# Late weight loads in held pieces, and a new instruction order, in an attention and gated-FFN kernel

## The chip, the cores and the metric

The kernel runs on one core of one Trainium2 chip. The metric is device time in microseconds; the time before is the median of three runs. Beside it stands one profiled execution, from which all durations of instructions come.

## The reference

One transformer block with adaptive layer norm, in bf16, for 2048 rows of width 448. Cut to what matters:

```python
mod = (silu(c) @ w_mod)                     # 448 -> 6 x 448: sa, ca, ga, sb, cb, gb
h = layernorm(x) * (1 + ca) + sa
x = x + ga * A(h)                           # attention, 16 heads of 28, 4 segments of 512 rows
h = layernorm(x) * (1 + cb) + sb
x = x + gb * B(h)                           # (sigmoid(h @ w_gate) * (h @ w_up)) @ w_down, 448 -> 1792 -> 448

# A, per segment s and head:
logits = q @ k.T * scale + causal mask;  a_dot = softmax(logits) @ v
a_mem = (phi(q) @ M) / (phi(q) @ z + 1e-6)  # memory of the segments before
o = g * a_mem + (1 - g) * a_dot             # g = sigmoid(beta)
M += phi(k).T @ v;  z += phi(k).sum(rows)   # then o @ wo
```

## The kernel before

The rows are four segments of 512, each of four tiles of 128. For each segment there are these stages: layer norm of x (`ln1`), projection to q, k and v (`proj`; QK at L861, V at L873), attention in pairs of head groups (`attention`: logits at L942, exp on ScalarE at L956 and L962, masks on VectorE or GpSimd at L972 and L969, probabilities times v, "PV", at L997), the update and the reading of the memory (`memory`: L905, reading at L1012), the output projection with the second layer norm (`wo_ln2`, L1064) and the FFN (`ffn`: gate/up at L1086, tanh at L1091, product at L1093, down at L1105). Segments overlap freely.

Nothing in this order is written by hand. Every piece of work is a node with a duration, dependencies, buffers ("slots") and a priority. `Graph.run` plays the nodes through a model of the five engines, takes at each moment the ready node of highest rank plus priority, and emits the instructions in the order found. The priorities are the long table `PRM`, one number for each node of a kind. So the instruction order on every engine changes when a number of the model or the table changes. Where the plan leaves TensorE (PE) idle for over 465 ns, `fillers` puts matmuls of an identity matrix (L1129, 512 columns) into the gap. They compute nothing that is used.

The model of transfers: `moved` gives each of two rings (SP's and ACT's queue) a time at which it is done, at `ALONE` bytes per ns for one ring and `SHARED` for each of two. A load of over 100,000 bytes isn't placed until its ring has less than `BACKLOG` ns left (`ready_at`). On the chip nothing enforces that: SP issues its instructions in order, each waiting only for its own inputs, for its buffers, and for the completion of an earlier DMA whose semaphore it reuses.

Weights, x and w_mod are loaded whole into SBUF by `load` (all at L470; `load_x`, `load_wm`, `load_half` call it). The first nine (x of segment 0, c, the first two sixths of w_mod in halves, wq and wk) are followed by x of segment 1, wv and the late loads: x of segments 2 and 3, wo, beta, the other four sixths of w_mod, w_gate and w_up, w_down. The late ones are 0.1 to 0.8 MB in one DMA each. wq and wk land in the room of w_down (`wqk_st`) and are copied into padded form (`pad`, L684), each half of the rows by itself. The modulation columns come from small matmuls (`mod_cols`, L647), rows of `rep` from L667; `rep` is multiplied into wo and w_down (`scaled`, L737).

SP's queue also carries the work of the pipeline: DMA transposes of phi(k) for the memory (`pk`, L897), of normalized x to hT (L746; segments 1 and 2 of the first norm are transposed on PE instead, L801), shifts of hT by half a partition range (L763, L766), and the stores (L1114). All of them stand in one order with the loads.

Of the kernel before, what the change touches and what calls it, by code (L numbers as in the profile page):

```python
# [13 lines left out]
P = 128  # L14
# [5 lines left out]
BACKLOG = 4000  # L20
SLACK = 250
INF = float("inf")
ALONE, SHARED = 245.0, 128.0

PRM = {
    "ld": (369044, 307344, 893451, -617209, 30545, -391681, 769994, 478104, 1506413, 246196, -153238, 622995, -344888,
        224457, 782907, 740955, -44415, -487957, -94697, 242376, -73834, 194363),
    "ws": (-205973, 384123, 102965, -72595, 270215, -214773, -562464, -199188, 289943, -1205891, -728759, -1210279,
        -853673, -1075673, -350090, -1112115, -456678, -2097630),
    "pj": (-809354, -799212, -1778232, -1222127, -1304831, -1422717, -1211794, -1974074, -2582402, -1784797, -1731699,  # L30
        -1432997, -787233, -1335907, -2169951, -2822676, -1343114, -2573680, -1822391, -2040683, -923550, -2107391,
        -2184641, -1772924, 241705, 15, 907154, 1122271, 852108, -24519, -377776, -196722, -768290, -3128, -829073,
        1122250, 558630, -504600, 262888, 119667, 425019, 241126, -781718, 138521, -173254),
    "ev": (910059, 583732, 734901, 348841, 415278, 361124, 390341, -350495, 605466, 1248190, 724478, 252990, 351177,
        -1060760, 99560, -339224, -579824, -480446, -952199, -1451478, -1228059, -1526733, -1188205, -2509101,
        1191510, 22486, -84708, -371324, -169064, -114692, -190608, -244213, 362489, -343011, -1096591, -1537722,
        -1239794, -971924, -673075, -1689010, -798158, -1411682, -1153882, -1348954, -1025849, -1118869, 14420,
        -1271712),
    "ln1": (52067, 457878, 689734, -177302, 167731, 288133, 181471, 312244, 85018, -190473, 836826, 733058, 908845,
        372065, 683673, -149642, 344424, 242833, 314959, 501854, 448238, 419745, 542826, -964768, -865865, -230782,  # L40
        109468, 724418, 41927, 192489, 345817, 251112, 277411, 939082, 576541, -160264, -329797, 306498, 897168,
        766275, 2031348, 501806, 1766664, -69744, -39732, 324817, 229652, -54789, 3426, 289366, 830871, -47867,
        504740, 17973, -332856, -194935, -270092, 657322, -1107999, 525892, -759213, -396386, 733594, 749680, 106946),
    "lg": (1903571, 2022275, 1868112, 2492143, 2383876, 2586210, 2118683, 1882073, 2434369, 1886752, 1265668, 1340630,
        739152, 1303984, 1344026, 2536971, 1764119, 1241619, 1417148, 940850, 2512247, 2373585, 1883725, 1755289,
        2246130, 2550777, 1280778, 1713172, 2980793, 1929447, 297802, 204360, 890058, 334188, 793051, -100783, 18628,
        609572, 158909, 686064),
    "ex": (3564046, 3415132, 3230920, 3886453, 2313177, 2404922, 3927356, 3471590, 4587747, 4505003, 1453103, 1197683,
        1419481, 1801405, 2800617, 2386818, 3055996, 2191047, 3943526, 3948848, 560113, 365875, 32592, -221844,
        348045, 873648, 6784, -481362, -603239, 302311, 769230, 1239061, 267867, 1564753, 637563, 638151, 281869,  # L50
        1036958, -746944, -317314),
    "mask": (949863, 968922, 1025971, 1653190, 2119047, 1920918, 1193528, 1060185, 968830, 1168662, 761261, 2129529,
        312432, 868757, 101127, 1364527, 250510, 1113337, 577913, 1276705, -40254, 536688, 1489338, 1029585, 1609834,
        1409696, 1024136, 1708955, 1607140, 1259647, 859837, 927495, 2427991, 2719449, 1857647, 2000572, 2270880,
        2012462, 1984328, 1632846, 1905041, 2121280, 2009590, 1692404, 1761962, 1685634, 1411239, 2185621, 793486,
        1192963, 1059030, 2141224, 1191945, 832868, 1583163, 551125, 210455, 441087, 634838, 930737, -10241, 608473,
        -235122, -86120),
    "pv": (2024955, 1705170, 2121590, 2726403, 185538, -734262, -103118, 865308, 606370, 149540, -254295, 990181,
        1635364, -434629, 60743, -536729),
    "t": (4021845, 3284741, 3378831, 2837695, 3791130, 4028739, 3373723, 4088406, 4456495, 4394824, 4316511, 4464689,  # L60
        3610155, 4144735, 3351270, 3974440, 3926537, 3705196, 4153703, 3844887, 12885, 665101, 305886, 211984,
        -280121, -239218, -459123, -25417, -320069, -238085, -287382, -666766, -111888, -448350, 124538, -369246,
        -737071, -213905, 1061166, -157374, -171996, -1478, -128551, -487876, 557914, 87380, -870478, 593318, 1660752,
        1126315, 1432537, 1325506, 1564262, 1782156, 1087670, 323061, 1594629, 2449642, 1918056, 2171760, 1574669,
        2005941, 1301827, 463032, 1435304, 1616727, 1524119, 1834373, 1839720, 1166831, 1239971, 1945109, 1293771,
        563554, 691509, 578776, -1494877, -458256, -787761, -824978, -1302790, -1050010, -1163239, -485195, -1937716,
        -1556847, -1977134, -1339590, -1591507, -1970508, -2635238, -2513520, -2630457, -2795043, -1814184, -1961049,
        -2590543, -2115038, -2828279, -2902843, -1841705, -1839436, -1490899, -2503918),
    "mem": (-761151, -31405, -1250643, -869816, -54841, -648031, -672042, -515182, -241137, -578229, -847415, -707828,
        -701013, -644854, -766583, -909362, -815994, -721421, -1269986, -748082, -793279, -932656, -656490, -671383,  # L70
        -536295, -654941, -333962, -463382, 380173, -204560, -289039, 209087, 66392, 502939, 1382865, -131351,
        -234499, 66498, 1231588, -58380, 599180, 376114, 33108, 526362, -607611, -195402, 218825, -912746, 360064,
        375098, 307889, 1040252, -29441, -60290, -266616, -302473, -408987, 589363, -40653, 114816, 45042, -209977,
        -1122178, 261467, -391896, -1074153, 480972, -311029, -174412, -372529, -189426, -300491, 544003, -226374,
        -196848, -136121, -149339, 611266, -694186, 132091, -189423, 189256, 125668, 100891),
    "wo": (1549545, 297144, 804041, 702070, 1410707, 1336115, 626526, 817071, 2184614, 2146397, 2195436, 3865766,
        -25540, 876630, -102149, -105363),
    "ln2": (1332947, 1273028, 1506731, 1286904, 124566, 995769, 1035016, 1551617, 1637288, 2670502, 1260360, 1672705,
        1429596, 1478613, 1276621, 1000534, 1279013, 729179, 2058679, 539528, 1161654, 664944, 1389903, -89914,
        1278040, 378904, 3125799, 2357638, 2948912, 3377722, 3084159, 1860920, 3172458, 4033052, 3001611, 3242704,  # L80
        3029696, 2951538, 3082954, 4190512, 4732975, 3146788, 3328802, 3364689, 3878089, 3501800, 3192639, 4423838,
        3895319, 3861042, 4240208, 3567222, 1208624, 928648, 1364166, 1658632, 1079427, 1126380, 804122, 330511,
        1687289, 665380, 16347, 868165, 774465, 1536304, 414383, 1917025, 1747624, 748313, 540321, 1319646, 1356096,
        2538213, 2029661, 1858805, 2001187, 1359124, -1285087, -2150644, -1723686, -1460713, -1619459, -1822046,
        -2048580, -2655047, -1898342, -2398157, -1965591, -2604854, -1591466, -2787155, -2631412, -2568863, -2435621,
        -3364265, -3599030, -2755780, -3191395, -3312191, -3255869, -2777146, -1945181, -2783150),
    "gu": (1883258, 2529781, 1813290, 2063698, 2907212, 2816880, 2759594, 3435519, 3657375, 4012953, 2379677, 3091622,
        2629540, 2690560, 4073697, -9991, 586451, 230677, -63569, 57047, 1016820, 159005, 1337820, 1174721, 600366,
# [23 lines left out]
        212024, 797709, -654264, -1385151, -216052, -431657, -526471, -392088, -1414877, -1357692, -1196457, -826264,  # L112
        -938840, -867425, -1377686, -1389691, -861918, -1830229, -1270960, -572877, -769492, -1156832, -2091094),
}
STAY = 84351
COST = {"ACT": 1.136, "DVE": 1.482, "POOL": 0.978}


# [220 lines left out]
def kernel(  # L339
# [17 lines left out]
    _, S, D = A_x.shape  # L357
# [805 lines left out]
```

## Time and profile before

| | |
|---|---|
| runs | 260.26, 261.92, 262.08 us; median 261.92 |
| profiled execution | 260.36 us, its span 258.6 us |
| mean granted PE clock | 0.993 |
| busy in the span | PE 238.2 us, VectorE (DVE) 196.7, ScalarE (ACT) 155.1, GpSimd (POOL) 36.8 |
| HBM | 11.07 MB read, 1.84 MB written |

Lines of a profile name the kernel's line, the engine, the operation and "out<-in" tiles; "x28" is a count; a bracket at the end is the time its engine stood idle before it and what ended that. In a timeline the first two numbers are start and length in us. The busy time of pipelined matmuls is modelled.

### The profile page before, as it was taken

The numbers are of one execution on the slowest core, as the hardware profiler recorded it, in microseconds if no ns is written. First come the engines' busy times: TensorE is split into PE (matmuls) and PEld (weight loads), VectorE is DVE, ScalarE is ACT, GpSimd is POOL, SyncE is SP. The second block draws the span as 40 slices with busy tenths as digits, with TensorE's granted clock in tenths as the row PEclk, the third lists the DMA queues.
The fourth block names the chain that finished last, engine by engine and source line by source line (L and its number), as shares of the span: only waits on it lengthen the run. The fifth ranks groups of instructions, "written<-read, shape, count | busy, mean of one in ns | idle before, by whom it ended". The sixth has DMA issues, their size and how long they took to land. (4 is left out here: it accounts for less than half of the span.)

```text
span 258.6 us, 6013 instructions
## 1 busy us (share of the span) xinstructions
PE 238.2 (92%) x2397; PEld 107.7 (42%) x2397; DVE 196.7 (76%) x499; ACT 155.1 (60%) x195; POOL 36.8 (14%) x91
## 2 busy tenths in 40 slices
PE   8769889979897999998979999899999999999994
PEld 3534545623332444433424444344444444454442
DVE  4489989987999998799998996669898754332431
ACT  5039969969988868898476558777431223022300
POOL 6204052300610000012500160000001300000000
PEclk9999999979999999999999999999999999999999
DMA  6999999993433010101354015201100330100011
GB/s 166 208 220 216 216 174 241 227 160 62 114 63 94 20 24 0 23 4 20 77 68 103 4 29 73 71 3 35 38 0 0 63 92 4 53 18 3 0 37 37
DMA packets 29832, 19.78 MB, mean 76 GB/s; under 512 B 18347, under 2 KB 28268, under 8 KB 29804
## 3 DMA queue, kind: packets, MB, share of 16 engines
q1 hardware_dynamic: 29276, 18.77, 36.5%
q10 hardware_dynamic: 528, 0.63, 0.9%
q8 instruction: 19, 0.31, 0.5%
q14 instruction: 9, 0.07, 0.1%
HBM read 11.07 MB, written 1.84 MB: 50 GB/s over the span
## 5 line engine op out<-in xcount | busy, mean ns | idle before, releaser
L1086 PE MATMUL ps<-hT,wgu 64*128 64x512 bf16 x784 | 91.2, 377 | 2.7 <-DMA hT<-hT 1.3
L1091 ACT ACTIVATE tt<-ps 128x512 f32<-128x512 f32 x56 | 33.5, 597 | 58.9 <-PE ps L1086 56.5
L956 ACT ACTIVATE pT<-ps 128x2048 bf16<-128x2048 f32 x32 | 60.4, 1886 | 6.9 <-PE ps L942 6.9
L1086 PEld LDWEIGHTS <-wgu 64*128 64x128 bf16 x784 | 38.8, 94 | 50.8 <-issue 13.1
L1093 DVE SCALAR_TENSOR_TENSOR fT<-tt,ps 128x512 bf16<-128x512 f32 x56 | 38.1, 682 | 25.9 <-ACT tt L1091 25.8
L1105 PE MATMUL ps<-wd_sb,fT 128*128 128x448 bf16 x224 | 46.2, 353 | 0.0
L861 PE MATMUL ps<-hT,wqk 64*128 64x512 bf16 x224 | 28.1, 383 | 2.5 <-DVE hT L821 1.9
L1105 PEld LDWEIGHTS <-fT 128*128 128x128 bf16 x224 | 20.4, 98 | 22.7 <-issue 5.7
L969 POOL TENSOR_SCALAR_AFFINE_SELECT pT<-pT 128x512 bf16<-128x512 bf16 x17 | 10.9, 638 | 95.1 <-DVE aT L1020 39.7
L972 DVE TENSOR_TENSOR pT<-pT,cmask 128x512 bf16<-128x512 bf16 x47 | 18.4, 419 | 6.8 <-ACT pT L956 5.6
L595 DVE BATCH_NORM_STATS2 st<-x_sb 128x6 f32<-128x448 bf16 x32 | 19.7, 615 | 3.9 <-DMA x_sb<-in_A_x_dram 3.5
L603 POOL TENSOR_TENSOR rs<-rs,mhalf 128x1 f32<-128x1 f32 (+1 forms) x29 | 17.0, 586 | 2.4
L861 PEld LDWEIGHTS <-wqk 64*128 64x128 bf16 x224 | 10.7, 94 | 14.9 <-issue 5.5
L942 PE MATMUL ps<-qT,kT 28*128 28x512 bf16 (+3 forms) x256 | 16.1, 304 | 0.4 <-DVE hT L821 0.2
L602 POOL TENSOR_SCALAR rs<-mv 128x1 f32<-128x1 f32 (+1 forms) x29 | 6.6, 226 | 68.8 <-DVE mv L596 61.5
L1112 DVE TENSOR_TENSOR ot<-ps,x_sb 128x448 bf16<-128x448 f32 x16 | 9.8, 618 | 8.5 <-PE ps L1105 8.2
L962 ACT ACTIVATE pT<-ps 128x2048 bf16<-128x2048 f32 x8 | 15.0, 1877 | 0.9 <-PE ps L942 0.9
L997 PE MATMUL ps<-pT,vt 128*32 128x512 bf16 (+3 forms) x256 | 12.0, 302 | 2.1 <-DVE x_sb L1067 0.8
L1064 PE MATMUL ps<-wo_sb,oT 128*128 128x448 bf16 x64 | 13.3, 353 | 0.4 <-DVE wo_sb L737 0.2
L844 ACT CAST kT<-ps 128x512 bf16<-128x512 f32 x12 | 7.1, 593 | 8.0 <-PE ps L861 8.0
L608 DVE TENSOR_SCALAR xn<-x_sb,mv,rs 128x448 bf16<-128x448 bf16 x32 | 11.4, 389 | 0.6 <-POOL rs L603 0.5
L873 PE MATMUL ps<-wvv,hT 64*128 64x448 bf16 x112 | 11.8, 350 | 0.0
(95 smaller groups left out, 240.4 us busy)
## 6 DMA issues: line engine op xcount, KB each, us to landing
out_dram<-ot SPq DMA_DIRECT2D x16, 112.0 KB, 1.7
wgu<-in_B_w_gate_dram SPq DMA_DIRECT2D x3, 448.0 KB, 11.4
wgu<-in_B_w_up_dram SPq DMA_DIRECT2D x3, 448.0 KB, 16.0
hT<-hT SPq DMA_DIRECT2D x5, 256.0 KB, 3.2
hT<-hT SPq DMA_DIRECT2D x5, 192.0 KB, 2.7
x_sb<-in_A_x_dram SPq DMA_DIRECT2D x2, 448.0 KB, 15.6
wd_sb<-in_B_w_down_dram SPq DMA_DIRECT2D x2, 448.0 KB, 11.4
wvv<-in_A_wv_dram SPq DMA_DIRECT2D x2, 392.0 KB, 8.1
```

The costliest lines, as they stand in the source:

```text
L595: nc.vector.bn_stats(st_r[:, st.at, :], src)
L603: nc.gpsimd.tensor_tensor(r, r, mhalf[:, 0:w], ALU.pow)
L861: nc.tensor.matmul(pf(b), lhsT=w, rhs=piece(hT, i, half), start=(i == 0), stop=(i == NP - 1))
L942: nc.tensor.matmul(ps[:, lg.at + hs, o:o + nq], lhsT=kT_r[r, k.at, hcs[u], kb * P:(kb + 1) * P], rhs=qT_r[r, q.at, hcs[u], kb * P:L], star ...
L956: nc.scalar.activation(pT_r[:, pTs[units[0]].at, :, w0:w0 + L], ps_, AF.Exp, scale=scale)
L962: nc.scalar.activation(dst, ps_.rearrange("p h (u w) -> p u h w", u=2), AF.Exp, scale=scale)
L972: nc.vector.tensor_tensor(blk, blk, cmask[:].rearrange("p (o k) -> p o k", o=1).to_broadcast([P, 4, P]), ALU.mult)
L1064: nc.tensor.matmul(pf(b)[:, 0:D], lhsT=oT_r[:, oT.at, k, t * P:(t + 1) * P], rhs=wo_sb[:, k, :], start=(k == 0), stop=(k == NHC - 1))
L1086: nc.tensor.matmul(pf(b), lhsT=wgu[half * HR:(half + 1) * HR, chunk_of(i, half), fs], rhs=piece(hT, i, half), start=(i == 0), stop=(i == N ...
L1091: a = act(485, lambda gp=gp, tt=tt: nc.scalar.activation(tt_r[:, tt.at, :], pf(gp), AF.Tanh, scale=0.5), [n], use=[gp, tt], prio=pr("tanh" ...
L1093: f = dve(597, lambda up=up, tt=tt, ft=ft: nc.vector.scalar_tensor_tensor(fT_r[:, ft.at, :], tt_r[:, tt.at, :], 1.0, pf(up), op0=ALU.add, ...
L1105: nc.tensor.matmul(pf(b)[:, 0:D], lhsT=fT_r[:, fts[fc].at, t * P:(t + 1) * P], rhs=wd_sb[:, fc, :], start=(fc == 0), stop=(fc == NFC - 1))
```

## The change

Three edits, and what follows from them.

1. `load` ties each load from the tenth on to the third load ahead of it in the order of creation: it is a dependency of the node in the plan, and on the chip a semaphore wait of the issuing queue until that load has landed.
2. The late loads are cut into pieces: x in halves of a segment, w_mod in two or four pieces, w_gate and w_up by one chunk of 64 rows at a time (0.23 MB), w_down by two chunks (0.23 MB). Their order of creation is also changed.
3. The model's rates are lower (215 and 111 for 245 and 128), the backlog limit is taken out (the tie stands in its place), rings start at 2000 ns for 2600, the lags of the first loads are other ones, and `PRM`, `STAY` and `COST` are all new. So the order of instructions is another one on every engine.

The number of instructions of each kind stays, but for loads and for fillers (14 to 41). A few evacuations, modulations, masks and scalings move between ACT, DVE and POOL.

```diff
-BACKLOG = 4000
+BACKLOG = 1e9
...
-ALONE, SHARED = 245.0, 128.0
+ALONE, SHARED = 215.0, 111.0
...
-STAY = 84351
-COST = {"ACT": 1.136, "DVE": 1.482, "POOL": 0.978}
+STAY = 96324
+COST = {"ACT": 0.957, "DVE": 0.883, "POOL": 0.756}
...
-        self.ring = {"SP": 2600.0, "ACT": 2600.0}
+        self.ring = {"SP": 2000.0, "ACT": 2000.0}
...
             n.fn(n.eng) if len(n.durs) > 1 else n.fn()
+            if n.move is not None:
+                n.name = block[was].name
+            if n.tie is not None:
+                tc.add_manual_dep(block[was], n.tie.name, mybir.DependencyInfo(
+                    mybir.DependencyClass.Sync, mybir.DependencyReason.DATA), reason="few loads wait at a time")
...
-    EARLY, LATE = -1500, 1200
+    EARLY, LATE = -900, 500
+    DEPTH, UNTIED = 3, 9
+    loads = []
...
-        return add(eng, 450 if size < 200000 else 640, fn, deps, prio=prio, use=use, take=take, move=size, lag=lag)
+        tie = loads[-DEPTH] if len(loads) >= UNTIED else None
+        n = add(eng, 450 if size < 200000 else 640, fn, [*deps, tie], prio=prio, use=use, take=take, move=size, lag=lag)
+        n.tie = tie
+        loads.append(n)
+        return n
...
-                    HR * (c1 - c0) * n * 2 * 1.15, (), prio, lag=lag)
+                    HR * (c1 - c0) * n * 2 * 1.03, (), prio, lag=lag)
...
-    W_qk = [load_half("SP", wqk_st, half, w, first(6 + half), lag=-200) for half, w in enumerate((A_wq, A_wk))]
+    W_qk = [load_half("SP", wqk_st, half, w, first(6 + half), lag=900) for half, w in enumerate((A_wq, A_wk))]
...
-    load_x("SP", 2 * TPS, 3 * TPS, ld())
-    load_wm(("SP",), 2, 1, fT_flat[:, 2 * NK * D:], ld())
+    load_x("SP", 2 * TPS, 2 * TPS + 2, ld())
+    load_x("SP", 2 * TPS + 2, 3 * TPS, ld())
...
-    load_wm(("SP",), 3, 2, fT_flat, ld())
-    W_gu = [load_half("SP", wgu, half, w, ld(), c0, c1) for c0, c1 in ((0, 2), (2, 4), (4, 6), (6, 7))
-            for half, w in ((0, B_w_gate), (1, B_w_up))]
-    load_x("SP", 3 * TPS, 4 * TPS, ld(), [n_warm, n_pads, *n_vpad, *n_vone, *n_opad])
-    load_wm(("SP",), 5, 1, fT_flat[:, 3 * NK * D:], ld())
+    load_wm(("SP", "SP"), 2, 1, fT_flat[:, 2 * NK * D:], ld)
+    W_gu = []
+
+    def load_gu(c0, c1):
+        for c in range(c0, c1):
+            W_gu.extend(load_half("SP", wgu, half, w, ld(), c, c + 1) for half, w in ((0, B_w_gate), (1, B_w_up)))
+    load_gu(0, 2)
+    load_wm(("SP",) * 4, 3, 2, fT_flat, ld)
+    load_gu(2, 4)
+    load_x("SP", 3 * TPS, 3 * TPS + 2, ld(), [n_warm, n_pads, *n_vpad, *n_vone, *n_opad])
+    load_x("SP", 3 * TPS + 2, 4 * TPS, ld(), [n_warm, n_pads, *n_vpad, *n_vone, *n_opad])
+    load_gu(4, NC)
+    load_wm(("SP", "SP"), 5, 1, fT_flat[:, 3 * NK * D:], ld)
     l_wd = []
-    for f0, f1 in ((0, 4), (4, 7), (7, 11), (11, 14)):
-        l_wd += [load("SP", wd_sb[:, f0:f1, :], B_w_down.rearrange("(fc p) n -> p fc n", p=P)[:, f0:f1, :],
-                      (f1 - f0) * P * D * 2, W_p if f0 < NC else (), prio=ld())] * (f1 - f0)
+    for f0 in range(0, NFC, 2):
+        l_wd += [load("SP", wd_sb[:, f0:f0 + 2, :], B_w_down.rearrange("(fc p) n -> p fc n", p=P)[:, f0:f0 + 2, :],
+                      2 * P * D * 2, W_p if f0 < NC else (), prio=ld())] * 2
```

The changed kernel's lines stand 12 to 20 further down than the old ones (the QK matmul, L861 before, is L881 after).

## The prediction

> **What bounds the kernel now.** I read the page first, then timelines of TensorE (PE), VectorE (DVE), ScalarE (ACT) and the SyncE queue (SPq), then windows.
>
> ```profile
> span 258.6 us, 6013 instructions
> ...
> PE 238.2 (92%) x2397; PEld 107.7 (42%) x2397; DVE 196.7 (76%) x499; ACT 155.1 (60%) x195; POOL 36.8 (14%) x91
> ...
> GB/s 166 208 220 216 216 174 241 227 160 62 114 63 94 20 24 0 23 4 20 77 68 103 4 29 73 71 3 35 38 0 0 63 92 4 53 18 3 0 37 37
> ```
>
> PE is busy for 92% of the span; the loads run at some 216 GB/s (slices of 6.5 us) until 57 us. The window from the first tanh of the gate/up stage (83.95) to the end shows the rest (columns: length; busy PE, weight load, DVE, ACT, POOL; clock, DMA share, GB/s):
>
> ```profile
> 83.95:258.60 174.65, 166.72 (x1544) 73.05 (x1540) 126.14 (x290) 91.98 (x112) 14.42 (x32) 1.00 0.15 33
> ```
>
> Of 174.65 us PE is idle 7.93, and 3.36 of those follow the last matmul. So this stage is PE's, and loads can matter only ahead of 84 us. There PE shows these waits for transposes (pk) that share the SP queue and its DMA engines with the loads:
>
> ```profile
> 52.31 0.28 PE L905 MATMUL ps<-vt,pk 128*32 128x32 bf16 x16 [0.42 <-DMA pk<-pq]
> ...
> 54.31 0.28 PE L905 MATMUL ps<-vt,pk 128*32 128x32 bf16 x16 [1.40 <-DMA pk<-pq]
> ...
> 67.65 0.28 PE L905 MATMUL ps<-vt,pk 128*32 128x32 bf16 x16 [0.68 <-DMA pk<-pq]
> ```
>
> The transpose for the 54.31 line was issued at 47.99, 6.3 us earlier, behind loads; the page's median for all twelve is 3.4 us. After that idle time PE's granted clock (after the busy time in these rows) fell:
>
> ```profile
> 56.00:57.00 1.00, 1.00 (x8) 0.50 0.71 86
> 57.00:58.00 1.00, 1.00 (x7) 0.50 0.60 128
> ```
>
> The microseconds beside these stand at 0.75 and 0.55, so the clock cost 0.25 + 0.5 + 0.5 + 0.45 = 1.7 us. What loads cost through transposes is thus 2.5 us of waiting and 1.7 of clock: at most 4.2 us to be gained.
>
> **Part 1, the start.** The changed order (compared instruction by instruction) moves three things ahead of the first query/key matmul (QK). Before:
>
> ```profile
> 8.76 2.63 PE L801 MATMUL ps<-ident,xn 128*128 128x128 bf16 x32
> 11.23 2.03 PE L647 MATMUL ps<-silu,pT 112*128 112x32 bf16 x64
> 13.11 0.81 PE L1129 MATMUL ps<-ident 128*128 128x512 bf16 x3
> 15.79 0.61 PE L861 MATMUL ps<-hT,wqk 64*128 64x512 bf16 x4 [1.88 <-DVE hT L821]
> 16.67 3.18 PE L861 MATMUL ps<-hT,wqk 64*128 64x512 bf16 x26 [0.27 <-ACT hT L823]
> ```
>
> The 32 transposes (L801) use the time in which w_mod is still landing (issued 1.72 and 2.02, 7.8 and 7.9 us to landing: 9.92). In the changed order 32 of the 64 column matmuls stand ahead of the transposes, so PE stands still until 9.95. Then 32 columns 1.0 (half of 2.03), transposes 2.6, 32 columns 1.0: 14.5. DVE's columns 0.2 and semaphores: hT begins at 14.8 (15.20 before), and its five parts with ACT's two between take 3.1 as before (15.20 to 18.32): 17.9. Now the second move: DVE copied two of wk's four pads before hT (14.28, 0.69 for two); now all four follow hT, so QK starts at 17.95 + 0.35 + 0.1 = 18.4, not 15.79. Third, 14 fillers (idle matmuls that the order puts in PE gaps, 0.20 each by 0.81 for three with overlap, 0.21) fill 14.5 to 17.4, inside the wait, so they cost nothing; without that cover 2.9. Before, the first two heads' QK came in bits as hT landed, the first exp began at 20.63. Now 28 QK (26 in 2.98 at 20.14, so 3.2) and 0.3 logits give 22.1, with the same lead to exp **22.5: 1.9 us late**. DVE is not late: its pads and zeroing were done meanwhile.
>
> **Part 2, up to the first gate/up.** ACT between 20.63 and 83.95 is busy 56.2 and idle 7.2 (63.32 less 56.16 in the window). Counting ACT's order in the same stretch, the changed one has 2 exps more (1.77 apart by their starts), 5 evacuations fewer (0.48), 1 e, 1 hT and 1 epsilon evacuation fewer (0.53, 0.70, 0.58), both LN multiplies gone to other engines (0.72 each), one small tanh more: 3.5 - 2.4 - 1.8 - 1.4 + 0.1 = -2.0. So 22.5 + 54.2 + 7.2 = **83.9**, with the waits as before. PE's order gives bounds. I sum it by groups with their spacing in dense rows (QK and gate/up 0.1155 each, V 0.105, 0.33 a group of logits, 0.66 for 16 PV, wo 0.196, filler 0.21): 57.2 us from the first QK to the end of the first 14 gate/up (24 fillers in them), 56.4 before (10 fillers). Before, 67.9 us passed (15.8 to 83.7), 11.5 over the work. 18.4 + 57.2 + 11.5 = 87.1 if nothing is saved; less 2.9 for 14 more fillers that stand where waits were, and less the 4.2 above, 80.0. ACT's value lies between and I take it.
>
> **Part 3, the loads.** 38 pieces now go out by SP after the first ones, each waiting for the third ahead of it. A 112 KB load landed in 2.4 to 2.6 us; 0.2 MB more than that at 216 GB/s gives some 3.0, three in flight: 1.0 us a piece, 0.2 MB/us, near the 216 of before. From x of segment 1 (now held until w_mod lands, 9.9; DVE needs it at 19) the list runs to 55 to 59 us; before it ended at 57. I cost it at nothing up to 84 us; cover: x of segment 3, W_gate/up and W_down are needed after 50, 80 and 110 us. Behind each held piece in SP's queue stand pk transposes (four, between pieces) and then eight hT transposes; DVE gives their inputs at about 40, 41, 48, 52 and 60 us (its work summed in its new order, plus the 8 to 10 us by which DVE lags its own sum in the old one), which is what SP will wait for. Bounds: at 1.29 us a piece (37.5 us from 14 to 51.5 over 29 pieces) the queue is late for the second w_mod load that rep needs, and each 0.1 above costs 2.9 us. Below, pieces can gain the 4.2 us already counted.
>
> The Trainium skill speaks against pieces: "DMA: Bandwidth & Descriptors", Rules for kernel authors, wants 1 MiB a transfer for full rate and small ones joined. Its fixed 2.0 us plus bytes at 436 GB/s (Anatomy of one DMA) makes an estimate of 2.5 us a piece, 0.84 with three in flight, so the same page's figures say the list isn't slowed; by the bare rule it would be, and the sum would be the queue rival's.
>
> **Part 4, the work that is left.** At the end of the first 14 gate/up matmuls the old order has done 28 V matmuls (2.93 at 46.40), 16 memory (0.21) and 4 read matmuls (0.28) more; the new one 16 PV (0.66) and 2 logits groups (0.33 each) more. That is 3.4 - 1.3 = **2.1 us more PE work left**, and one filler more: 2.3. Everything from here on is PE's as shown, with 4.57 of idle time inside it. I take it as equal; bounds -2.5 (the 1.81 us wait for a pk transpose at 135 and the 0.94 at 121 to 123 go) and +3 (as much again at the new cluster of memory and PV matmuls). DVE's sum rises by about 1.1 us and ACT's falls by 3; neither ends last here.
>
> **Sum.** 83.9 - 83.95 + 2.3 = +2.2 on a profiled run of 260.36 us (span 258.6 and 1.8 around it). That run lies 1.56 under the median of 261.92, so on the scale of the runs **264.1 us**.
>
> The skill's page "TensorE: Matmul & The Clock Gate" (The HAM clock gate) has the clock halve after an idle window of about 3.4 us. The trace shows it after 1.82 us of idle time in 3 us (52.3 to 55), and not after 1.88 at 13.9. By the rule PE's stillness from 7.0 to 9.95 costs nothing; by the row it may cost up to 1.7.
>
> **The rivals.**
> - *Transposes freed (faster).* No pk transpose waits behind more than three pieces, the clock holds, and the point is 80.0; the later pk wait goes too: -3.9 + 2.3 - 1.8 = -3.4, **258.5**. For it: the three waits and the half clock. Against: QK and ACT start late, and 22 fillers ahead of gate/up say that the order itself expects PE to wait there. It decides if the point lies before 81.
> - *The SP queue holds (slower).* At 1.6 us a piece the list is 9 us late for rep and the hT transposes behind it: **273**. For it: 0.45 MB loads took 11 to 16 us to land. Against: those stood in a long queue. It decides from 1.29 us a piece.
> - *Absorbed (no change).* The 2.3 us of PE work left fill idle time that DVE's or ACT's pace causes after 84 us: 4.57 shrink by 2.3: **261.9**. Against: PE is 100% busy in most of that stretch.
> - That the hold does nothing can't be: SP's list shows a wait ahead of every late piece. If loads land at the same times, the new order still stands, and that is the forecast.
>
> **Chances.** A difference of 1% (2.6 us) is about what a measurement here tells. Forecast 0.50 (its own range 261.5 to 268: half within 1%, half slower); freed 0.22 (0.20 faster); held 0.15, slower; absorbed 0.13 (0.02 faster). Faster 0.22, same 0.38, slower 0.40. The range goes from just under the freed rival's time (258.0) to 269.0, over the forecast's +3 and half-way to the held queue's price.
>
> **What would show it.** Right: QK starts at 18 to 18.8 with no PE work from 7 to 9.9; first exp near 22.5; first tanh of gate/up at 82 to 86; load landings of about 3 us, the last load landed before 62; pk waits on PE under 1 us together before 70; clock whole at 56 to 59; after that tanh as much idle time as before. Wrong: the tanh before 81 or after 88; rep or a W_down product waiting for DMA; idle time after the tanh off by over 3 us.

## The result and the profile after

| | before | after |
|---|---|---|
| median of 20 runs | 261.88 us (257.82 to 264.27) | 263.0 us (261.64 to 265.49) |
| profiled execution, its span | 260.36 us, 258.6 us | 263.85 us, 262.1 us |
| mean granted PE clock in it | 0.993 | 0.987 |

The ratio of after to before is 1.0113, 95% interval 1.0075 to 1.015: about 1% slower. The ratios here use only the runs within 1.5% of the fastest of the same kernel, so they are not quotients of the medians; that quotient is 1.004 for this change. The two profiled executions lie 3.5 us apart, the medians 1.1: what follows splits the difference of these two executions.

From the page of the changed kernel: the span, the busy time of the engines, the granted clock and the transfer rate by slices of 6.6 us, and the loads with their size and time to landing.

```profile
span 262.1 us, 6080 instructions
...
PE 245.5 (94%) x2424; PEld 111.9 (43%) x2424; DVE 198.3 (76%) x497; ACT 152.5 (58%) x189; POOL 43.1 (16%) x99
...
PEclk9769999999999999999999999999999999999999
...
GB/s 142 203 174 135 193 208 191 165 216 198 41 85 90 41 34 0 42 105 67 22 23 42 54 18 3 21 63 77 48 0 18 83 70 3 36 35 3 0 38 35
...
wgu<-in_B_w_gate_dram SPq DMA_DIRECT2D x7, 224.0 KB, 3.3
```

A piece of w_gate lands in 3.3 us, where the loads of w_gate and w_up before, twice as large, took 11 to 16. But the rate over the list is lower (135 to 208 GB/s in slices 3 to 8, against 174 to 241), the list runs on through slice 10 (198 GB/s, against 62), and the clock fell in the two slices between 6.6 and 19.7 us.

The start on PE's timeline (start, length, what, and in brackets the idle time before it):

```profile
10.00 1.51 PE L659 MATMUL ps<-silu,pT 112*128 112x32 bf16 x32 [1.88 <-DMA pT<-in_w_mod_dram]
11.35 4.16 PE L821 MATMUL ps<-ident,xn 128*128 128x128 bf16 x32
15.30 1.30 PE L659 MATMUL ps<-silu,pT 112*128 112x32 bf16 x32
16.44 3.53 PE L1149 MATMUL ps<-ident 128*128 128x512 bf16 x14
19.91 3.20 PE L881 MATMUL ps<-hT,wqk 64*128 64x512 bf16 x28
```

The columns come first and stand until w_mod lands, as the order says. After that idle time the 32 transposes take 4.16 us instead of 2.63: half clock. QK starts at 19.91 (15.79 before).

The waits for pk transposes ahead of the last stage:

```profile
47.28 0.28 PE L925 MATMUL ps<-vt,pk 128*32 128x32 bf16 x16 [0.78 <-DMA pk<-pq]
...
52.75 0.27 PE L925 MATMUL ps<-vt,pk 128*32 128x32 bf16 x16 [1.00 <-DMA pk<-pq]
...
56.41 0.28 PE L925 MATMUL ps<-vt,pk 128*32 128x32 bf16 x16 [0.30 <-DMA pk<-pq]
...
80.37 0.28 PE L925 MATMUL ps<-vt,pk 128*32 128x32 bf16 x16 [0.83 <-DMA pk<-pq]
```

There are four instead of three, none longer than 1.0 us: 2.9 us in all (2.5 before), and the clock stays whole behind them. VectorE also waits once for a held piece of w_down, ahead of its scaling:

```profile
60.82 0.39 DVE L757 TENSOR_TENSOR wd_sb<-wd_sb,rep 128x448 bf16<-128x448 bf16 x1 [1.36 <-DMA wd_sb<-in_B_w_down_dram]
```

The first exp comes at 23.62, the first tanh of gate/up at 85.29. From there to the end:

```profile
85.29:262.10 176.81, 169.61 (x1565) 76.22 (x1564) 127.08 (x288) 90.93 (x115) 20.99 (x42) 1.00 0.17 36
```

Against the row of before (174.65 us, PE busy 166.72) this stretch is 2.16 us longer and PE has 2.89 us more to do in it; its idle time is 7.20 instead of 7.93. So in the two profiled executions the 3.5 us of loss in span are 1.34 ahead of that tanh and 2.16 behind it.

### The profile page after: what moved, and what is told of

It is laid out like the page before. It is cut to its first block, busy times and chain, and to the rows that moved or that the text cites. A ratio compares the mean times of both kernels' runs of the same rounds, so it can differ in the third digit from the quotient of the medians.

```text
span 262.1 us, 6080 instructions
## 1 busy us (share of the span) xinstructions
PE 245.5 (94%) x2424; PEld 111.9 (43%) x2424; DVE 198.3 (76%) x497; ACT 152.5 (58%) x189; POOL 43.1 (16%) x99
## 4 chain that ended last, share of the span: by engine, by line
PE 44%; DVE 29%; DMA 19%; issue 3%; ACT 2%; SPq 1%; POOL 1%; DVEq 0%; POOLq 0%; ACTq 0%
PE ps L1106 26%; PE ps L1125 10%; DMA wgu<-in_B_w_up_dram 4%; DMA pT<-in_w_mod_dram 3%; DVE x_sb L1087 3%; DVE st L607 3%; DMA hT<-hT 3%; DVE fT L1113 2%; DVE pT L992 2%; DMA fT<-in_w_mod_dram 2%; DVE A L1044 2%; PE ps L881 2%; DVE U L1059 2%; PE ps L1017 2%; PE ps L821 2%
## 5 line engine op out<-in xcount | busy, mean ns | idle before, releaser
L1106 PE MATMUL ps<-hT,wgu 64*128 64x512 bf16 x784 | 92.9, 377 | 2.6 <-DMA hT<-hT 1.4
L1106 PEld LDWEIGHTS <-wgu 64*128 64x128 bf16 x784 | 39.7, 94 | 49.3 <-issue 13.3
L881 PE MATMUL ps<-hT,wqk 64*128 64x512 bf16 x224 | 27.2, 377 | 0.3 <-DVE qT L866 0.3
L989 POOL TENSOR_SCALAR_AFFINE_SELECT pT<-pT 128x512 bf16<-128x512 bf16 x19 | 11.9, 636 | 58.3 <-ACT pT L976 28.9
L992 DVE TENSOR_TENSOR pT<-pT,cmask 128x512 bf16<-128x512 bf16 x45 | 17.4, 417 | 2.9 <-ACT pT L976 2.1
L881 PEld LDWEIGHTS <-wqk 64*128 64x128 bf16 x224 | 11.0, 94 | 13.1 <-issue 2.2
L1017 PE MATMUL ps<-pT,vt 128*32 128x512 bf16 (+3 forms) x256 | 11.4, 301 | 1.2 <-DVE pT L992 0.9
L843 ACT ACTIVATE hT<-ps,cols 128x512 bf16<-128x512 bf16 x5 | 4.0, 800 | 12.3 <-DVE cols L669 10.9
```

The lines of the kernel that those rows point to most:

```text
L881: nc.tensor.matmul(pf(b), lhsT=w, rhs=piece(hT, i, half), start=(i == 0), stop=(i == NP - 1))
L992: nc.vector.tensor_tensor(blk, blk, cmask[:].rearrange("p (o k) -> p o k", o=1).to_broadcast([P, 4, P]), ALU.mult)
L1017: nc.tensor.matmul(pf(acc)[hs * HP:(hs + 1) * HP, kb * P:L], lhsT=vt_r[:, v.at, kb, hc * 4 + hs, :], rhs=pT_r[:, pT.at, hs, OFF[kb]:OFF[kb ...
L1106: nc.tensor.matmul(pf(b), lhsT=wgu[half * HR:(half + 1) * HR, chunk_of(i, half), fs], rhs=piece(hT, i, half), start=(i == 0), stop=(i == N ...
```

## The experiments

Each was timed against the kernel before on the same chip. Times are medians of all runs; everything read from a timeline or a window is from one profiled execution. Edits are shown without the lines that only pass a node on (such as `G.mm0 = mm0`), and `...` marks what is left out of a line.

### The new order without the hold

```diff
-            if n.tie is not None:
-                tc.add_manual_dep(block[was], n.tie.name, ...)
```

> The changed kernel with the same order, the same pieces and the same plan, but without the wait of each load for the third one ahead; only the reuse of eight DMA semaphores still holds loads. Theory S (the loss sits in the order: the late start and the work left, the hold itself costs and gains little): ratio to the kernel before as the changed kernel's 1.011, within 0.004; loads land after 6 to 9 us instead of 3, and the four pk transposes of segment 0 wait 1 to 2 us longer on PE, first tanh of gate/up at 85 to 87. Rival H (the hold is what slows it, by keeping SP's queue waiting): ratio at or below 1.003. Rival T (the hold is what keeps pk transposes quick, so that it is worth something): ratio at or above 1.018.

Measured: 263.14 us, ratio 1.005 (1.001 to 1.009); landings of the weights' pieces 4.1 to 5.3 us. Tanh at 84.71, and 176.7 us from there to the end. The ratio lies between theory S and rival H, and its interval overlaps that of the changed kernel, so that the hold costs up to some 0.6% isn't ruled out. The list of loads isn't faster for it: 174 GB/s over 20 to 50 us, against 184 with the hold. SP's queue shows what holds the list instead:

```profile
31.47 0.47 SPq L475 DMA_DIRECT2D wgu<-in_B_w_up_dram  x1
38.75 1.30 SPq L914 DMA_TRANSPOSE pk<-pq  x1
```

The new order puts the first pk transpose among the pieces, and from 31.9 to 38.75 SP stands until VectorE has written its input pq, with the remaining pieces behind it.

### The new order with ten fillers ahead of the first columns

```diff
         fill = self.fillers(order)
+        fill[id(self.mm0)] = (fill[id(self.mm0)][0], 10)
```

> The changed kernel with 10 identity matmuls in place of 1 ahead of the first column matmuls, where PE stands still from 8.1 to 10.0 us and its clock then shows 0.50 from 11 to 17 us. Theory S with the clock as the part that the prediction missed: clock whole from 10 to 17, the 32 transposes take 2.6 instead of 4.2 us, QK starts at 18.2 to 18.6 instead of 19.9, first tanh of gate/up 1.0 to 1.5 us earlier, ratio about 1.006. Rival: the stretch from 20 to 85 us is bound by VectorE and ScalarE in such a way that a start earlier by 1.5 us is lost again: QK earlier, tanh still at 85.3, ratio 1.011.

Measured: 262.76 us, ratio 1.0049 (1.0009 to 1.009). In the profiled execution the clock is 1.000 throughout:

```profile
10.78 2.63 PE L823 MATMUL ps<-ident,xn 128*128 128x128 bf16 x32
...
17.31 3.30 PE L883 MATMUL ps<-hT,wqk 64*128 64x512 bf16 x28
```

With the clock whole QK starts 2.6 us earlier than in the changed kernel's profile, the first exp is at 21.02 and the tanh at 83.12. That is the start as the order has it; the rest of the 19.91 was clock. (The run without the hold and the one with fillers late in the last stage, both with the start unchanged, show a whole clock there and begin QK at 17.08 and 16.82: the halving comes in some executions only.)

### The new order with the old start

The 64 columns behind the transposes again, the two late pads ahead of hT, 8 fillers instead of 14:

```diff
+        qk = next(i for i, n in enumerate(order) if id(n) in fill and fill[id(n)][1] == 14)
+        fill[id(order[qk])] = (fill[id(order[qk])][0], 8)
+        for n in (self.mm0, self.sa):
+            order.remove(n)
+        i = order.index(self.mm1)
+        order[i:i] = [self.mm0, self.sa]
+        late = [self.pads[1], self.pads[3]]
+        for n in late:
+            order.remove(n)
+        i = order.index(self.pads[6]) + 1
+        order[i:i] = late
```

> The changed kernel with the start in the old order: the 32 transposes ahead of all 64 column matmuls, the two pads of wk for the first two groups of heads ahead of hT, 8 instead of 14 fillers ahead of QK. Theory S: QK starts at 15 to 16.5 us, its first 28 end by 19.5 instead of 23.0, first exp 3 to 4 us earlier, first tanh of gate/up 2.5 to 4 us earlier, ratio 0.996 to 1.002. Rival (the stretch up to 85 us is bound by the chain of loads, transposes and LN work rather than by its start): tanh less than 1 us earlier, ratio 1.007 to 1.011.

Measured: 264.13 us, ratio 1.0107 (1.0065 to 1.015): not what the theory said. QK starts at 15.76 and the first exp at 20.61, as before, but the tanh comes at 85.76:

```profile
37.19 0.21 PE L670 MATMUL ps<-silu,fT 112*128 112x32 bf16 x2 [1.06 <-DMA fT<-in_w_mod_dram]
...
39.20 2.97 PE L894 MATMUL ps<-hT,wqk 64*128 64x512 bf16 x14
```

PE now reaches the matmuls on the second part of w_mod before its held pieces are there, stands, and runs at half clock afterwards (14 QK in 2.97 us; whole, 1.69). Most of the 3.0 us gained at the start is lost at the next thing that the list brings: 1.06 us of waiting and, by the clock of the microseconds after it, some 1.7.

### The old order, its own loads held by three

```diff
+            if n.eng == "SP" and n.move is not None and n.move > 100000 and n.lag > 0 and "load" in n.fn.__qualname__:
+                sent.append(block[was].name)
+                if len(sent) > 11:
+                    tc.add_manual_dep(block[was], sent[-4], ...)
```

> The kernel before with its own order and its loads whole, and the hold alone added: on the queue each late load waits until the third one ahead of it in the order of issue has landed. Theory S (the hold is worth little): pk's wait on PE at 52 and 54 us falls from 1.8 to under 1 us, loads land after 5 to 8 us instead of 11 to 16, ratio 0.994 to 1.002. Rival T (the hold frees the transposes and keeps the clock): ratio 0.985 to 0.992. Rival H (SP stands waiting and the last loads are late): the last load lands after 62 us instead of 57, ratio above 1.005.

Measured: 261.89 us, ratio 1.0018 (0.998 to 1.0057): nothing. With pieces of up to 0.8 MB, three in flight keep the list at 213 GB/s (20 to 50 us; 214 before). Landings fall to 6 to 7.5 us, but PE still waits 1.83 us for a transpose.

### The new order without fillers

```diff
         fill = self.fillers(order)
+        fill = {}
```

> The changed kernel without its fillers (the matmuls on the identity that the planner puts into gaps of TensorE; their results are never read, so the output is the same). Theory that they stand where TensorE waits anyway and hold its clock: the first gate/up tanh no earlier than in the changed kernel (85.3 us), half clock after the empty 13 to 18 us and after the empty stretches at 72 to 83 us, where 21 of them stood; median 263.0 to 266, ratio to before 1.005 to 1.02. Rival, that they delay real work (27 more of them than before, 0.21 us each, up to 5.6 us): tanh 82 to 84 us, median 258 to 261, ratio 0.985 to 0.998.

Measured: 267.68 us, ratio 1.0247 (1.0178 to 1.0316). Behind waits that fillers had covered the clock is halved:

```profile
16.82 6.08 PE L882 MATMUL ps<-hT,wqk 64*128 64x512 bf16 x27 [1.86 <-DVE wqk L697]
...
80.67 0.30 PE L926 MATMUL ps<-vt,pk 128*32 128x32 bf16 x16 [2.15 <-DMA pk<-pq]
...
81.45 1.46 PE L1107 MATMUL ps<-hT,wgu 64*128 64x512 bf16 x6
```

27 QK take 6.08 us instead of 3.1, six gate/up 1.46 instead of 0.82. The tanh comes at 87.21, 1.9 us later than with fillers, and the clock of all six runs is 0.954 to 0.968 (0.979 to 0.998 with fillers). The rival, that the fillers delay real work, fell.

### The old order with fillers in two waits

```diff
+        fill[id(self.mems[1])] = (self.mems[1].take[0].at, 2)
+        fill[id(self.mems[2])] = (self.mems[2].take[0].at, 6)
```

> The kernel before with 2 and 6 fillers in the two waits for a transpose at 51.9 and 53 to 54.3 us, so that TensorE isn't still there. Theory that the half clock at 55 to 59 us is lost time: clock whole at 55 to 59 us, first gate/up tanh up to 1.7 us earlier (82.3 to 83.5), median 260.2 to 261.2 where before has 261.9, ratio 0.993 to 0.998. Rival, that VectorE and ScalarE set the tanh and TensorE waits for them a little later instead: clock whole, tanh at 83.7 to 84.5, ratio 0.999 to 1.003. If TensorE's fillers end later than the transposes land: slower by 0.2 to 0.5 us.

Measured: 261.21 us, ratio 0.9994 (0.9947 to 1.004). The half clock at 55 to 59 us is gone. In the profiled execution another came in its place, at a later wait:

```profile
80.45 4.22 PE L1090 MATMUL ps<-hT,wgu 64*128 64x512 bf16 x21 [1.09 <-DMA hT<-hT]
```

These 21 gate/up matmuls took 2.53 us before. So this run doesn't tell what the clock is worth; a later one tells more.

### The changed kernel with 12 fillers late in the last stage

```diff
+        late = next(n for n in order if n.eng == "PE" and n.start > 225000 and n.mode == "H" and n.take)
+        fill[id(late)] = (late.take[0].at, 12)
```

> The changed kernel with 12 fillers (0.21 us each, 2.5 us of TensorE work, results never read) ahead of a group of gate/up matmuls late in the last stage, where TensorE is never idle. Theory that after the first gate/up tanh each microsecond of TensorE work left is a microsecond of time: the stretch from that tanh to the end grows from 176.8 to 179.0 to 179.6 us, ratio 0.010 above that of the changed kernel (1.015 to 1.022). Rival, that work left is taken up by TensorE's idle time (7.2 us in this stretch): 176.8 to 177.8, ratio 1.005 to 1.012.

Measured: 266.17 us, ratio 1.0188 (1.0125 to 1.0251), and in its profile:

```profile
84.46:263.90 179.44, 172.24 (x1576) 77.23 (x1575) 127.04 (x288) 90.94 (x115) 20.98 (x42) 1.00 0.15 36
```

PE is busy 2.63 us more than in the changed kernel, and the stretch is 2.63 us longer. There, work left is time, one for one.

### The changed kernel without most of V of segment 3

```diff
                 for half, b in enumerate(b2):
+                    if s == NSEG - 1 and i:
+                        continue
```

> The changed kernel with 24 of the 28 V matmuls of segment 3 left out (six of the seven parts of its sum, so that segment's V and what follows from it are not the reference's). They stand after the first gate/up tanh in the changed kernel and ahead of it in the kernel before. 24 at 0.1 us are 2.4 us of TensorE work. Theory that the work moved behind that point is what the change loses: the stretch from the tanh to the end 174.2 to 174.9 us instead of 176.2 to 176.8, ratio 0.998 to 1.004. Rival, that VectorE or ScalarE fills the hole: 175.8 to 176.8, ratio 1.006 to 1.013.

Measured: 263.47 us, ratio 1.0057 (1.0016 to 1.0098). The ratio lies between the two theories. It is 0.0056 below that of the changed kernel, some 1.5 us of the 2.4 taken out, but the intervals overlap. The profiled execution took 266.36 us, 2.9 more than the median, so it shows what can fill the hole and not what the median does:

```profile
113.19 0.82 PE L881 MATMUL ps<-hT,wqk 64*128 64x512 bf16 x6 [1.28 <-ACT tt L1113]
...
121.21 1.86 PE L1108 MATMUL ps<-hT,wgu 64*128 64x512 bf16 x7 [1.97 <-DMA hT<-hT]
122.47 4.43 PE L881 MATMUL ps<-hT,wqk 64*128 64x512 bf16 x28
```

Where the V matmuls stood (107 us in the changed kernel), PE now waits for ScalarE's tanh, and then for the shift of hT, which ends that wait 35.4 us after the first tanh; in the changed kernel it ended 35.0 us after it, behind 0.94 us of idle time. The idle time is followed by half clock. The stretch from tanh to end is 178.8 us, of which the half clock at 120 to 126 us cost 1.7: without that it is 177.1, as long as in the changed kernel (176.81). So in this execution the hole was worth nothing, since another chain arrives at 120 us in any case. The expectation was not met: how much of the loss those matmuls make stays open, between nothing and some 1.5 us.

### The old order, late loads in pieces, each held by three

The order of before on all engines; only the form of the loads is the change's.

```diff
+            for a in range(0, dst.shape[1] if step else 1, step or 1):
+                z = slice(a, min(a + step, dst.shape[1])) if step else slice(None)
+                (nc.sync if eng == "SP" else nc.scalar).dma_start(dst[:, z, :] if step else dst, ...)
...
+                for i in range(was, len(block)):
+                    sent.append(block[i].name)
+                    if len(sent) > 11:
+                        tc.add_manual_dep(block[i], sent[-4], ...)
```

> The kernel before with its own order on all engines, but each late load sent as the changed kernel's pieces (pairs of tiles of x and W_down, single chunks of gate and up, two or four pieces of w_mod), each held until the third one ahead of it has landed. Only the form of the loads is changed. Theory that this form is worth nothing and the new order makes the loss: landings of 2.8 to 4 us, the list done 3 to 6 us later than before, tanh at 83.5 to 85, ratio 0.997 to 1.003, remainder after the tanh 174.4 to 175.0. Rival, that the form itself costs: transposes behind the held list late, tanh 85.5 to 88, ratio 1.006 to 1.015. Rival, that it gains what the waits and the half clock at 52 to 60 us cost and only the order loses it: tanh 80 to 82.5, ratio 0.985 to 0.995.

Measured: 266.28 us, ratio 1.0205 (1.0145 to 1.0266). My theory fell: the form is not worth nothing. In SP's queue the last held pieces and the first transposes behind them:

```profile
46.55 4.85 SPq L478 DMA_DIRECT2D wd_sb<-in_B_w_down_dram  x4
51.45 2.60 SPq L905 DMA_TRANSPOSE pk<-pq  x2
```

On PE's timeline, the wait for the first of them and what follows:

```profile
54.34 0.30 PE L913 MATMUL ps<-vt,pk 128*32 128x32 bf16 x16 [4.47 <-DMA pk<-pq]
54.57 2.80 PE L881 MATMUL ps<-wvv,hT 64*128 64x448 bf16 x14
```

The first transposes of pk go out behind the held pieces at 51.45, not at 42.94; PE stands 4.47 us, runs at half clock (14 V matmuls in 2.80 us; whole, 1.50), and the tanh comes at 89.22. After it 174.78 us, as before. This is the mechanism of the prediction's queue rival, in the old order, but with pk instead of rep as what waits, and at 191 GB/s over 20 to 50 us, some 1.1 us a piece, where the rival was to need 1.29.

### The same pieces without the hold, and held by six

Both edits are against the run above.

```diff
-                    if len(sent) > 11:
-                        tc.add_manual_dep(block[i], sent[-4], ...)
```

> The kernel before, its own order, with the late loads cut into the changed kernel's pieces but not held until the third one ahead of them has landed (each still waits for the eighth load ahead of it, as in the kernel before). Beside the run in which the pieces were held by three (ratio 1.0205, tanh at 89.2, first two transposes of pk issued at 51.45), this tells the cut from the hold. Theory that the hold by three slows the list and so delays what stands behind it in SP's queue: here the list ends 3 to 4 us earlier, the transposes are issued at 47.5 to 48.5, PE waits at most 2 us for one, tanh at 83.5 to 85, ratio 0.997 to 1.005. Rival, that small pieces are slow by themselves: transposes issued at 50.5 to 52, tanh at 87.5 to 90, ratio 1.013 to 1.022.

Measured: 261.52 us, ratio 0.997 (0.9921 to 1.0019). The cut costs nothing. In its profiled execution (262.77 us) loads landed in 6.3 to 9.8 us, the first pk transposes went out at 44.44, and PE still waited 0.68 and 1.39 us for a transpose.

```diff
-                    if len(sent) > 11:
-                        tc.add_manual_dep(block[i], sent[-4], ...)
+                    if len(sent) > 14:
+                        tc.add_manual_dep(block[i], sent[-7], ...)
```

> The kernel before, its own order, late loads in the changed kernel's pieces, each held until the sixth one ahead of it has landed instead of the third. With three pieces of 0.2 MB in flight and some 3.2 us to land, 3 times 0.2 MB in 3.2 us is 188 GB/s, below the 210 to 220 GB/s that the list runs at with eight in flight; with six it would be over them. Theory that the hold costs only where it keeps the list below that rate: loads at 205 GB/s or more up to 53 us, the third transpose of pk issued at 47.5 to 50.5 us, tanh at 83.5 to 86, ratio 0.996 to 1.005. Rival, that any hold delays SP's queue, because an instruction that waits keeps all behind it: tanh at 87 to 90, ratio 1.012 to 1.022.

Measured: 259.95 us, ratio 0.9926 (0.9889 to 0.9964): better than the theory, and faster than both kernels. From its page, a piece and its median landing:

```profile
wgu<-in_B_w_gate_dram SPq DMA_DIRECT2D x7, 224.0 KB, 5.4
```

Its window over most of the list (length; busy PE, weight load, DVE, ACT, POOL; clock, DMA share, GB/s):

```profile
20.00:50.00 30.00, 27.87 (x392) 15.44 (x388) 28.79 (x84) 28.23 (x35) 10.55 (x22) 1.00 1.04 226
```

The first transposes of pk in SP's queue:

```profile
41.33 2.60 SPq L905 DMA_TRANSPOSE pk<-pq  x2
```

And PE's one wait for a transpose of over 0.5 us:

```profile
50.78 0.28 PE L913 MATMUL ps<-vt,pk 128*32 128x32 bf16 x16 [0.83 <-DMA pk<-pq]
50.98 1.69 PE L869 MATMUL ps<-hT,wqk 64*128 64x512 bf16 x14
```

226 GB/s, where the same pieces held by three had 191 and without the hold 208. (The whole loads of before had 214, 221 and 219 in three executions, so a difference of this size between six and eight in flight isn't shown.) A piece of w_gate lands in 5.4 us, 7.8 without the hold. The first two transposes go out 22.3 us after the first exp, as before (42.94 - 20.63; 30.9 with the hold at three): this hold doesn't delay them. One wait of 0.83 us is left of the 2.5, and the clock is whole up to the tanh. From the first exp (19.01) to the tanh (79.87) pass 60.9 us; before, 63.3. The 1.6 us by which the exp itself is earlier are not the hold's: it began at 19.13 in the old order with fillers in two waits, and at 20.47 with fillers in all large waits. From the tanh to the end this execution took 176.1 us, 1.5 more than before, with half clock at 132 to 136 us, behind a wait of 2.16 us for another pk transpose. By ratio the gain over the run without the hold isn't settled: 0.9926 and 0.997, with intervals that overlap.

### The old order with fillers in all large waits

```diff
+        fill[id(self.mems[1])] = (self.mems[1].take[0].at, 2)
+        fill[id(self.mems[2])] = (self.mems[2].take[0].at, 6)
+        threes = [n for n in order if fill.get(id(n), (0, 0))[1] == 3]
+        for n, k in zip(threes, (11, 7)):
+            fill[id(n)] = (fill[id(n)][0], k)
```

> The kernel before with fillers in all its large waits of TensorE ahead of the last stage: 11 instead of 3 ahead of the first query/key matmul, 2 and 6 in the two waits for transposes, 7 instead of 3 ahead of the gate/up group that waits for hT. Theory that the clock's halving, which came at one or the other of these waits in some runs and not in others, is what spreads the runs of the kernel before: clock at 0.993 to 1.0 in nearly every run, median 259.0 to 260.8, ratio 0.988 to 0.996. Rival, that the last stage or VectorE and ScalarE set the time, whatever the clock does ahead of it: ratio 0.998 to 1.004.

Measured: 260.21 us, ratio 0.9876 (0.9834 to 0.9919): the lowest ratio here. By the medians of all runs it is 0.992, and 0.991 for the pieces held by six, so which of the two is faster isn't shown. The spread did not go: 256.8 to 262.76 us. Of its 12 runs seven have a clock of 0.997 or more; of the 29 runs of the kernel before beside it, two. This kernel and the new order with ten fillers at its start are the two whose profiled execution has a clock of 1.000 in the whole span, so they compare the orders with the clock out of the way, one execution each. The old order (tanh at 83.30):

```profile
83.30:256.90 173.60, 167.02 (x1544) 73.52 (x1540) 125.25 (x287) 91.98 (x112) 14.42 (x32) 1.00 0.15 33
```

The new one (tanh at 83.12):

```profile
83.12:259.60 176.48, 169.52 (x1565) 76.01 (x1564) 126.82 (x288) 91.00 (x115) 21.09 (x42) 1.00 0.16 36
```

Both reach the tanh at the same time. Behind it the new order takes 2.88 us more: 2.50 us more of busy PE and 0.38 us more idle time. The matmuls behind the tanh differ as the prediction counted them: 28 of V, 16 of memory, 4 of its reading and one filler more, 16 PV and 12 logits (two groups) fewer, 21 in sum. The medians of the two are 2.55 us apart, taken on two chips.

## Why the prediction was right, and where it was not

**Forecast.** 264.1 us, 2.2 more than before, against 263.0: 1.1 more by the medians of all runs, 2.9 by the ratio of 1.0113. The forecast's own mechanism, a first tanh at about the same time and more PE work behind it, is what the pair with whole clock shows: 0.2 us apart at the tanh, 2.9 behind it. The profiled pair, with its half clocks, has 1.34 ahead of the tanh and 2.16 behind it.

**Part 4, the work left: right in size and in the count, its cause not settled.** Predicted +2.3; the changed kernel shows 176.81 - 174.65 = +2.16 and the other executions of the new order with its fillers and all its work are at 176.2 to 176.7. The extra matmuls are those that the prediction counted, and PE is busy 2.50 us more with whole clock. That work left counts one for one is shown late in the stage. It is not shown for the V matmuls: leaving out 24 of them returned nothing in the profiled execution, where ScalarE and then the hT shift at 120 us end the next waits, and at most some 1.5 us by the ratio. What makes the excess, if V is taken out, stays open.

**Part 1, the start: two errors that partly cancelled.** QK was put at 18.4 and the exp at 22.5; measured 19.91 and 23.62. With whole clock they are at 17.31 and 21.02. The step that fails is that QK begins after the last pads: it began at 17.31 while they ran (16.97 to 18.25), and VectorE's part of hT took 2.35 us, so the order costs 0.4 us at the exp against the profile of before, not 1.9. (Where the clock is whole, the first exp comes at 19.0 to 20.6 in the old order and at 20.5 to 21.0 in the new, so the cost lies anywhere up to 2 us.) The other error is the clock: the stillness until 10.0 was given "up to 1.7" in a side sentence and nothing in the sum, and it moved QK by 2.6 us in the profiled execution. The page "TensorE: Matmul & The Clock Gate" of the Trainium skill (The HAM clock gate), by which an idle window of about 3.4 us is needed, was the rule that I let weigh against the row. In the profile of the changed kernel the row was right: 1.88 us of idle time at this place brought half clock. In the run without the hold 1.89 us at the same place did not.

**Part 2, up to the tanh.** From the first exp to the tanh I counted 54.2 of ScalarE's work and 7.2 idle, 61.4; the changed kernel has 61.67, 54.69 busy and 6.98 idle. That the idle time agrees is in part luck: I took the waits as before, but the half clock of before was gone and the waits were others, and with the old start it was 10.0. In the other runs of the new order with fillers it is 62.1 (exp at 21.02) to 65.2 (exp at 20.61): much of what the start gains is waited for later. The tanh lies at 83.1 to 85.8 in all of them that have fillers, inside the 82 to 86 given as right.

**Part 3, the loads: the cost of nothing fits, its reason was wrong.** Landings of 2.8 to 3.8 us against "about 3.0", and whole clock at 56 to 59 us, as said. (A piece is 0.11 MB larger than the 112 KB load, not 0.2; the 3.0 comes out with 0.11.) But a piece was reckoned at 1.0 us, "near the 216 of before", and the list ran at 184 GB/s from 20 to 50 us; its last piece went out at 61.7, so that it landed after 62. Three pieces of 0.2 MB over some 3.3 us are 0.18 MB/us; the prediction's own 0.2 MB/us was already below the 216 that it was called near to. That this cost little I put down to the new order, which sends the pk transposes at 40.7 to 52.6 between pieces; in the old order the same form costs 2%. Of the signs given as right, four failed: QK and the first exp (Part 1), PE's waits for pk before 70 us, 2.1 us together and not under 1, and the last landing after 62. One sign given as wrong came: VectorE waited 1.36 us for a piece of w_down. The rule cited against pieces, 1 MiB a transfer ("DMA: Bandwidth & Descriptors", Rules for kernel authors), isn't tested at its size, as the loads of before are 0.1 to 0.8 MB; pieces of 0.2 MB in their place cost nothing, with a ratio of 0.997 and 208 GB/s against 214. The estimate of 2.5 us a piece by the same page's figures (Anatomy of one DMA), which it gives for DMAs issued by GpSimd, was below the 2.8 to 3.8 us measured for these, issued by SP.

**The rivals.** *Transposes freed* did not come with this change, but its mechanism is seen in the old order: with the hold at six the waits ahead of the tanh shrink to 0.83 us and the kernel takes 259.95 (the rival had 258.5). *The SP queue holds* came in the old order with the hold at three, 266.28 (the rival had 273, from a dearer piece, and for rep instead of pk). *Absorbed* fell: idle time behind the tanh did not shrink by the 2.3 us, only by 0.7, and with whole clock it grew by 0.38.

**The spread of the runs** goes with the clock in the changed kernel: of its 20 runs the two with a clock of 0.979 took 265.0 and 265.5 us, the eleven with 0.993 or more 261.6 to 263.2. The clock isn't all of it: the four runs of the old order with fillers in all large waits that have a clock of 1.000 took 258.65 to 262.76 us.

## What to carry to other kernels

A hold on loads has a depth, and depth times piece over landing time is a bandwidth: in the old order three pieces of 0.2 MB were too few (191 GB/s) and six kept the list full (226), with the shorter waits that the change was after. In the new order taking the hold away did not speed the list, since transposes that wait for their inputs stand in the same queue. A change of form and a new order made for it are two changes: try the form in the old order, and the order without the form, before either is credited or blamed. And the fillers in TensorE's waits earn their place: without them the changed kernel's ratio rises from 1.011 to 1.025, and with more of them the kernel before becomes 1.2% faster (0.8% by the medians of all runs).

## What was not expected of the hardware

- Halving of PE's clock after about 1.9 us of idle time is not a fixed rule of these executions. At the wait ahead of the first QK, 1.88 us (before) left it whole; 1.92 us (loads held by three) and 2.16 us (pieces held by three) did not: 22 QK in 4.90 us, 30 in 5.11. At the gate/up group, 1.09 us of idle time was enough once (21 matmuls in 4.22 us), and 1.00 us at the same place left the clock whole in the kernel before.
- Fewer loads in flight need not be slower: with the same pieces in the same order, six in flight moved 226 GB/s over 20 to 50 us, eight 208, three 191, each in one execution. That six is faster than eight isn't shown: eight whole loads in flight moved 214, 221 and 219.

The two best versions, the pieces held by six (0.9926) and the fillers in the waits (0.9876), were not run together; whether their gains add is open.
